# One array for K and V, read in tiles of 7 to 9 places across the borders of K, V and batches

## The chip, the cores and the metric

The kernel runs on one core of a Trainium2 chip. The metric is the device time of one execution in microseconds (us), as a median of runs. The engines named below are TensorE (PE, with PEld for its weight loads), VectorE (DVE), ScalarE (ACT), GpSimd (POOL) and SyncE (SP), which here does nothing but start DMA transfers from HBM to the on-chip memory. Everything is float32.

## The reference

Two rounds of the same pair of layers are applied to 8 batches of one token each: cached attention with 32 query heads on 4 K/V heads, then a GELU network. Both rounds use the same cache and the same weights, so every byte of K, V and the weights is used twice.

```python
B, Sq, D = 8, 1, 1024;  Hq, Hkv, Sk, Dh = 32, 4, 4096, 128;  F = 3584
def _A_ref(x, k_cache, v_cache, wq, wo):
    q = (x @ wq).reshape(B, Sq, Hq, Dh).transpose(0, 2, 1, 3)
    k = jnp.repeat(k_cache, rep, axis=1); v = jnp.repeat(v_cache, rep, axis=1)
    scores = jnp.einsum("bhqd,bhkd->bhqk", q, k) * (Dh ** -0.5)
    o = jnp.einsum("bhqk,bhkd->bhqd", _softmax(scores, axis=-1), v)
    return o.transpose(0, 2, 1, 3).reshape(B, Sq, Hq * Dh) @ wo
def _B_ref(x, w1, b1, w2, b2):
    return jnp.einsum("bsf,fd->bsd", _gelu(jnp.einsum("bsd,df->bsf", x, w1) + b1), w2) + b2
x = A_x
for _ in range(2):
    x = x + _A_ref(_layernorm(x, axis=-1), A_k_cache, A_v_cache, A_wq, A_wo)
    x = x + _B_ref(_layernorm(x, axis=-1), B_w1, B_b1, B_w2, B_b2)
```

## The kernel before

**Memory.** One on-chip tile, the arena, has 52 *places* (`N_UNIT`) of 1024 float32 columns in all 128 partitions, 512 KB each (`SCW`). K of one batch is 16 places, V is 16 places. A transfer fills k neighbouring places from a given first place. The first 28 places hold wq through layer 0, because layer 1's queries are made from the same copy; places 28 to 51 turn over.

**The stream.** All transfers stand in one list, `stream`, in the order in which they will be used, each with its size and its first place written out by hand. `pump` (L272) starts transfers from the head of the list for as long as the places of the next one are free; `release` (L287) frees a tile's places and pumps again. All of them are issued by SyncE on one queue, and a DMA instruction waits, in the program, for the last reader of the places that it overwrites.

```python
def pump():
    while stream:
        key, k, src, starts, keys = stream[0]
        ...
            slot = arena.take(k, [i for i in starts if i + k <= arena.limit])
        if slot is None:
            return
        stream.pop(0)
        nc.sync.dma_start(out=slot.ap[:, 0:src.shape[1]], in_=src)
```

**The order of the work.** Layer 0: wq (q0), then for batch 0 to 7 K and V in tiles of 8 and 4 places; the last V (of batch 7) in pieces of 1, 7, 4 and 4 places, of which the last 15 places stay for layer 1; then wo (o0), w1 (i0) and w2 in tiles of 1 to 4 places. Layer 1 takes the batches as 7, 6, ... 0: K of batch 7 and of batch 6 in small tiles, everything after that in tiles of 8 at places 26, 34 and 18 in turn, then wo (o1: 8, 8, 8, 4, 2, 2), w1 (i1: five of 4, three of 2, then 1, 0.5, 0.5) and the last three pieces of w2 (`LATE`, at place 20).

**The compute.** In `attention`, `scores` (L612) multiplies a pair of places of K with the queries; after 8 pairs `probs` does the softmax with VectorE and ScalarE (L617 to L643); `values` (L657) multiplies the pairs of V, VectorE picks the diagonal blocks (L660, L662), and `heads` (L669) puts the heads in place. `project` (L439) is the product with wo. `expand` (L317, L320) is the product with w1; a unit there is 8 row blocks of 512 columns, which is 4 places, and 7 units make the hidden layer. After half of the first unit it runs the variance of the layer norm (L211, L240), which the scaling of every unit (L335) needs; `hidden_wide` (L413, L417, L429) transposes a unit and applies the GELU. In layer 1 the contraction with w2 (`down_row`, L497) of each unit is woven in behind the next unit's matmuls, and the last thing is the sum on VectorE (L872) and the store.

A transfer's matmuls wait for the whole transfer. Each float32 matmul stands twice in the trace's counts.

Of the kernel before, what the change touches and what calls it, by code (L numbers as in the profile page):

```python
# [21 lines left out]
CH = 512  # L22
# [3 lines left out]
NG = W // CH  # L26
T = CH // P
NR = NH * HKV
EPS = 1e-5
PAD = 24  # L30
SCALE = DH ** -0.5
# [18 lines left out]
        ("w2", 7, 4, 0, 16), ("w2", 8, 4, 16, 8), ("w2", 9, 4, LAST, 4), ("x", 4), ("q", 4, 0), ("q", 4, 1),  # L50
        ("w2", 10, 5, 0, 16), ("q", 5, 0), ("w2", 11, 5, 16, 12), ("q", 5, 1), ("x", 5), ("q", 6, 0),
        ("w2", 11, 6, 0, 4), ("w2", 12, 6, 4, 16), ("q", 6, 1), ("w2", 13, 6, 20, 8), ("x", 6))
LATE_AT = 20
LATE_C = 2
LATE = ((0, 2), (2, 1), (3, 1))
NGR = F // CH
# [56 lines left out]


@with_exitstack
def decode_layers(ctx: ExitStack, tc: tile.TileContext, x, kc, vc, wq, wo, w1, w2, out):


    nc = tc.nc
# [480 lines left out]
    def v_at(b, r):  # L600
        return b, r // NH, r % NH
# [72 lines left out]

    def ap_of(key):

        parts = pieces[st["layer"], key] if (st["layer"], key) in pieces else pieces[0, key]
        chunks = [held[name].ap[:, c:c + CH] for name, c0, n in parts for c in range(c0, c0 + n, CH)]
        return chunks, [name for name, c0, n in parts if c0 + n == held[name].cols]

    def plan(order):

# [64 lines left out]
    def lane(layer, b, a, r, m):
        where = k_at if a == "k" else v_at
        keys = [(a, *where(b, e)) for e in range(r, r + m)]
        for e, key in enumerate(keys):  # L750
            pieces[layer, key] = [((layer, keys[0]), e * W, W)]
        return (layer, keys[0]), (kc if a == "k" else vc)[b][:, r * W:(r + m) * W]

    def cache(layer, b, a, at):
        r = 0
        while r < NR:
            n, starts = at(2 * (NR - r))
            name, src = lane(layer, b, a, r, n // 2)
            yield (name, n, src, starts, ())
            r += n // 2  # L760

    rsum = row_sums()
    nc.vector.tensor_reduce(rsum, x_row, AX.X, ALU.add)

    last_b = B - 1
    shared = (("v7", 1, 44), ("v7b", 7, 28), ("v7c", 4, 35), ("v7d", 4, 39))
    orders = [list(range(B)), list(range(B))[::-1]]

    def fixed(*at):
        return lambda k, i: (at[i],)  # L770
# [8 lines left out]
    def listed(*spots):
        spots = iter(spots)  # L780
        return lambda left: next(spots)

    def batch(layer, b, k_spots, v_spots):
        for a, spots in [(a, spots) for a, spots in (("k", k_spots), ("v", v_spots)) if spots]:
            stream.extend(cache(layer, b, a, listed(*((n, (at,)) for n, at in spots))))
# [3 lines left out]
    batch(0, 0, ((8, 40), (4, 32), (4, 36)), ((4, 28), (8, 40), (4, 32)))
    batch(0, 1, ((4, 36), (4, 28), (8, 40)), ((8, 32), (8, 40)))  # L790
    cycle = [(((8, 36), (4, 44), (4, 28)), ((8, 32), (8, 40))), (((8, 28), (4, 36), (4, 40)), ((4, 44), (8, 28), (4, 36))),
             (((8, 40), (8, 28)), ((4, 36), (8, 40), (4, 28))), (((8, 32), (8, 40)), ((8, 28), (4, 36), (4, 40))),
             (((4, 44), (8, 28), (4, 36)), ((8, 40), (8, 28)))]
    for b in orders[0][2:last_b]:
        batch(0, b, *cycle[(b - 1) % 5])
    batch(0, last_b, cycle[(last_b - 1) % 5][0], ())
    at = 0
    for name, k, to in shared:
        keys = [(1, name, e) for e in range(k)] if at else ()
        stream.append(((0, name), k, vc[last_b][:, at:at + k * SCW], (to,), keys))  # L800
        for e in range(k):
            key = ("v", *v_at(last_b, (at + e * SCW) // W))
            pieces.setdefault((0, key), []).append(((0, name), e * SCW, SCW))
            pieces.setdefault((1, key), []).append(((1, name, e), 0, SCW) if keys else ((1, name), 0, SCW))
        at += k * SCW
    weights(("o0",), wo[0], [3, 2] + [3] * 9, fixed(*[46, 49, 43] * 4))
    weights(("i0",), w1[0], [2] + [3] * 8 + [2], fixed(*[43, 46, 49] * 4))
    down_weights()
    stream.append((("qe", 0), 0, wq[0][:, -W:-KEEP], x_row[:, 0:W - KEEP], ()))
    stream.append(((1, "v7"), 1, vc[last_b][:, 0:SCW], (17,), ()))  # L810
    batch(1, last_b, ((2, 20), (2, 22), (4, 24), (2, 18), (2, 20), (2, 22), (2, 24)), ())
    batch(1, last_b - 1, ((2, 26), (2, 18), (4, 20), (2, 24), (2, 28), (4, 30)), ((8, 34), (8, 18)))
    at = [26, 34, 18] * (4 * B)
    for b in orders[1][2:]:
        batch(1, b, *([(8, at.pop(0)), (8, at.pop(0))] for _ in "kv"))
    weights(("o1",), wo[0], [8, 8, 8, 4, 2, 2], fixed(26, 34, 18, 26, 30, 32))
    weights(("i1",), w1[0], [4] * 5 + [2] * 3 + [1, 0.5, 0.5], fixed(34, 38, 18, 22, 26, 30, 32, 34, 36, 37, 38))
# [7 lines left out]
    for layer in range(2):  # L825
        st["layer"] = layer
        b2_row = spare[:, SCW:SCW + Q4]
        hooks = {("probs", last_b): opened} if layer == 0 else {
            ("v", *v_at(last_b - 2, 0)): lambda: bias_row(b2_row, spare[:, SCW + Q4:SCW + Q4 + CH]),
            ("v", *v_at(last_b - 1, 1)): rebuild,  # L830
            ("v", *v_at(last_b - 3, 0)): bias_diag,
            **{("k", *k_at(last_b, r)): lambda: unread(2) for r in range(NR - 4, NR)}}
        last = attention(orders[layer], hooks)
        rsum = row_sums()
        project(f"o{layer}", oT, x_row, rsum, {4: last})
        rs = layernorm(x_row, rsum)
# [76 lines left out]
def _start(x, b1, b2):  # L913
# [3 lines left out]

_LAYOUT = {
    'x': (('A_x', 'B_b1', 'B_b2'), _start),
    'k': (('A_k_cache',), lambda a: a.reshape(B, HKV, 4, 32, NH, W // DH, DH).transpose(0, 6, 4, 1, 2, 5, 3).reshape(B, P, -1)),  # L920
    'v': (('A_v_cache',), lambda a: a.reshape(B, HKV, P, -1).transpose(0, 2, 1, 3).reshape(B, P, -1)),
    'wq': (('A_wq',), _queries),
    'wo': (('A_wo',), _down),
    'w1': (('B_w1',), _across),
# [24 lines left out]
```

## Time and profile before

| | us |
|---|---|
| median of 3 runs (846.3 to 846.95) | 846.91 |
| profiled execution, whole | 849.2 |
| its span in the trace | 847.3 |
| TensorE busy in the span | 557.7 (66%) |
| VectorE busy | 193.4 (23%) |
| ScalarE busy | 55.9 (7%) |
| share of the 16 DMA engines that SyncE's queue took | 99.0% |

The span is the time from the first to the last instruction in the trace. Busy shares are averages over stages that have different limits, so the stages are read apart. In the chain of work that ended last the page puts 68% on DMA and 28% on TensorE.

### The profile page before, as it was taken

The numbers are of one execution on the slowest core, as the hardware profiler recorded it, in microseconds if no ns is written. First come the engines' busy times: TensorE is split into PE (matmuls) and PEld (weight loads), VectorE is DVE, ScalarE is ACT, GpSimd is POOL, SyncE is SP. The second block draws the span as 40 slices with busy tenths as digits, with TensorE's granted clock in tenths as the row PEclk, the third lists the DMA queues.
The fourth block names the chain that finished last, engine by engine and source line by source line (L and its number), as shares of the span: only waits on it lengthen the run. The fifth ranks groups of instructions, "written<-read, shape, count | busy, mean of one in ns | idle before, by whom it ended". The sixth has DMA issues, their size and how long they took to land.

```text
span 847.3 us, 9962 instructions
## 1 busy us (share of the span) xinstructions
PE 557.7 (66%) x4350; PEld 188.9 (22%) x4350; DVE 193.4 (23%) x642; ACT 55.9 (7%) x118; POOL 2.4 (0%) x14
## 2 busy tenths in 40 slices
PE   0756475566656647688988796576765566665778
PEld 0211121111111112133244322121211111112335
DVE  0013131313223231300010343231314132222011
ACT  0110000000000000000210200000000000000021
POOL 0000000000000000000000000000000000000000
PEclk9977778867787877799999998867688877878679
DMA  9999999999999999999999999999999999999997
GB/s 402 420 424 429 433 422 425 438 425 434 422 430 438 422 439 420 418 414 416 411 407 411 411 409 432 435 429 431 429 433 428 435 431 428 435 425 431 424 425 283
DMA packets 21066, 356.97 MB, mean 421 GB/s; under 512 B 2336, under 2 KB 2720, under 8 KB 4256
## 3 DMA queue, kind: packets, MB, share of 16 engines
q1 hardware_dynamic: 20880, 356.20, 99.0%
q8 instruction: 34, 0.56, 0.3%
q10 hardware_dynamic: 144, 0.15, 0.1%
q14 instruction: 8, 0.07, 0.0%
HBM read 356.21 MB, written 0.13 MB: 421 GB/s over the span
## 4 chain that ended last, share of the span: by engine, by line
DMA 68%; PE 28%; DVE 1%; issue 1%; another core or an unknown queue 1%; ACT 0%; SPq 0%; ACTq 0%; DVEq 0%
DMA arena<-in_k_dram 27%; DMA arena<-in_v_dram 24%; PE sps L612 8%; PE o_ps L657 8%; DMA arena<-in_w_dram 6%; DMA arena<-in_wo_dram 6%; DMA arena<-in_wq_dram 5%; PE acc L376 2%; PE acc L317 2%; PE sps L497 1%; PE y L439 1%; PE sps L484 1%; PE none L195 1%; PE sps L669 1%; PE acc L320 1%
## 5 line engine op out<-in xcount | busy, mean ns | idle before, releaser
L612 PE MATMUL sps<-arena,qz 128*32 128x512 f32 x1024 | 168.7, 801 | 120.2 <-DMA arena<-in_k_dram 119.1
L657 PE MATMUL o_ps<-arena 128*32 128x512 f32 x512 | 88.6, 811 | 44.3 <-DMA arena<-in_v_dram 32.8
L657 PE MATMUL o_ps<-arena,spare 128*32 128x512 f32 x512 | 81.4, 746 | 37.4 <-DMA arena<-in_v_dram 35.1
L612 PEld LDWEIGHTS sps<-arena,qz 128*32 128x32 f32 x1024 | 38.7, 136 | 211.0 <-issue 176.4
L662 DVE SCALAR_TENSOR_TENSOR scr<-o_ps,bits,scr 128x128 f32<-128x128 f32 x192 | 67.4, 351 | 6.8
L660 DVE TENSOR_SCALAR scr<-o_ps,bits 128x128 f32<-128x128 f32 x64 | 22.5, 351 | 135.9 <-PE o_ps L657 135.9
L439 PE MATMUL y<-arena,oxT 128*32 128x256 f32 x512 | 38.4, 444 | 18.1 <-DMA arena<-in_wo_dram 18.1
L669 PEld LDWEIGHTS sps<-bits,scr 128*128 128x128 f32 x128 | 22.0, 216 | 70.1 <-issue 49.1
L376 PE MATMUL acc<-arena,oxT 128*32 128x512 f32 x248 | 33.2, 664 | 6.5 <-DMA arena<-in_wq_dram 4.2
L657 PEld LDWEIGHTS o_ps<-arena 128*32 128x32 f32 x512 | 17.2, 134 | 79.3 <-issue 49.3
L195 PE MATMUL sps<-spare,ident 128*32 128x512 f32 (+2 forms) x82 | 33.9, 533 | 1.1 <-DVE scr L231 0.6
L670 DVE TENSOR_TENSOR oxT<-sps,scr 128x8 f32<-128x8 f32 x64 | 10.6, 165 | 101.1 <-PE sps L669 101.1
L617 DVE TENSOR_SCALAR_CACHE_REDUCE arena<-sps 128x512 f32<-128x512 f32 x16 | 11.1, 692 | 90.8 <-PE sps L612 90.8
L657 PEld LDWEIGHTS o_ps<-arena,spare 128*32 128x32 f32 x512 | 17.2, 125 | 65.4 <-issue 45.4
L638 ACT ACTIVATE sps<-arena,bits 128x512 f32<-128x512 f32 x16 | 10.9, 681 | 283.5 <-DVE scr L632 283.5
L617 DVE TENSOR_SCALAR_CACHE_REDUCE spare<-sps 128x512 f32<-128x512 f32 x16 | 11.1, 692 | 79.8 <-PE sps L612 79.8
L317 PE MATMUL acc<-arena,oxT 128*32 128x512 f32 x160 | 26.7, 675 | 3.8 <-DMA arena<-in_w_dram 3.8
L638 ACT ACTIVATE sps<-spare,bits 128x512 f32<-128x512 f32 x16 | 10.9, 681 | 266.1 <-DVE scr L632 266.1
L669 PE MATMUL sps<-bits,scr 128*128 128x8 f32 x128 | 27.9, 290 | 0.0
L439 PEld LDWEIGHTS y<-arena,oxT 128*32 128x32 f32 x512 | 17.2, 126 | 40.6 <-DMA arena<-in_wo_dram 24.0
L626 PE MATMUL sps<-scr,bits 128*128 128x128 f32 x32 | 7.4, 312 | 21.4 <-DVE scr L622 21.4
L220 PE MATMUL sps<-ident,xb 128*128 128x128 f32 x6 | 1.5, 344 | 24.2 <-DMA xb<-in_x_dram 23.2
(138 smaller groups left out, 285.3 us busy)
## 6 DMA issues: line engine op xcount, KB each, us to landing
arena<-in_v_dram SPq DMA_DIRECT2D x24, 4096.0 KB, 21.9
arena<-in_k_dram SPq DMA_DIRECT2D x22, 4096.0 KB, 21.3
arena<-in_k_dram SPq DMA_DIRECT2D x15, 2048.0 KB, 18.2
arena<-in_v_dram SPq DMA_DIRECT2D x10, 2048.0 KB, 18.6
arena<-in_wo_dram SPq DMA_DIRECT2D x10, 1536.0 KB, 9.8
arena<-in_w_dram SPq DMA_DIRECT2D x10, 1536.0 KB, 8.5
arena<-in_w_dram SPq DMA_DIRECT2D x12, 1024.0 KB, 9.8
arena<-in_w_dram SPq DMA_DIRECT2D x6, 2048.0 KB, 21.9
```

The lines of the kernel that those rows point to most:

```text
L195: nc.tensor.matmul(ps[0:32, 0:w], ident[:, 0:32], ap[:, 0:w], start=True, stop=True)
L317: nc.tensor.matmul(acc[32 * j:32 * j + 32, :], lhs, slot.ap[:, c:c + CH], start=(kt < 4), stop=(kt >= NT - 4))
L376: nc.tensor.matmul(acc[u][32 * j:32 * j + 32, d0 - j * CH:d1 - j * CH], xnT[:, kt * XS:kt * XS + 32], ap[:, d0 - c0:d1 - c0], start=(kt == ...
L439: nc.tensor.matmul(y[32 * j:32 * j + 32, 0:Q4], lhs[:, n * B:n * B + 32], slot.ap[:, c + j * Q4:c + (j + 1) * Q4], start=(n == 0), stop=(n ...
L612: nc.tensor.matmul(ps[32 * g:32 * g + 32, :], qz[:, c:c + 32], kt[g], start=(j == 0), stop=(j == HKV - 1))
L617: nc.vector.tensor_scalar(st["row", b].ap[:, half * CH:(half + 1) * CH], ps, SCALE, None, op0=ALU.mult, op1=ALU.max, accum_out=st["mx", b] ...
L638: nc.scalar.activation(pp, row[:, h * CH:(h + 1) * CH], AF.Exp, bias=bias, scale=1.0, accum_out=ls[:, h:h + 1])
L657: nc.tensor.matmul(o[32 * g:32 * g + 32, :], s[:, g], v[g], start=(half == 0), stop=(half == NH - 1))
L660: nc.vector.tensor_scalar(r, o[:, 0:P], sel_t[:, 0:1], None, op0=ALU.mult)
L662: nc.vector.scalar_tensor_tensor(r, o[:, t * P:(t + 1) * P], sel_t[:, t:t + 1], r, op0=ALU.mult, op1=ALU.add)
L669: nc.tensor.matmul(po[:, 0:REP], r_s[j % 2], sel_h, start=True, stop=True)
L670: nc.vector.tensor_tensor(oT_v[:, j * REP:(j + 1) * REP, b], po[:, 0:REP], rl_s[b % 2][:, j * REP:(j + 1) * REP], ALU.mult)
```

## The change

K and V, before two arrays with a pitch of 64 KB from one partition's row to the next, become one array `kv`: for every batch 16 places of K and 16 of V, all in one row of 256 places per partition, and one place of padding at the end of the row. A tile may hold any run of places, so that it can cross from K to V and from one batch to the next. `ap_of` now looks up the pieces of a pair place by place.

Layer 0 reads tiles of 8, 7 and 8 places at 36, 44 and 28 in turn. Layer 1 takes batch 7 first, as before, and then 0, 1, ... 6; after the small tiles it reads 9, 9 and 8 places at 34, 17 and 26 in turn. o1 is four tiles of 8; i1 is 8, three of 4, three of 2, 1, 0.5 and 0.5; `LATE_AT` goes from 20 to 22. The hooks that rebuild x and lay out the biases stay at the second, third and fourth batch of layer 1's order.

```diff
-LATE_AT = 20
+LATE_AT = 22
...
-        parts = pieces[st["layer"], key] if (st["layer"], key) in pieces else pieces[0, key]
-        chunks = [held[name].ap[:, c:c + CH] for name, c0, n in parts for c in range(c0, c0 + n, CH)]
-        return chunks, [name for name, c0, n in parts if c0 + n == held[name].cols]
+        parts = [part for _, part in sorted(pieces[st["layer"], key].items())]
+        chunks = [held[name].ap[:, c + e:c + e + CH] for name, c in parts for e in range(0, SCW, CH)]
+        return chunks, [name for name, c in parts if c + SCW == held[name].cols]
...
+    def cache(layer, g, spots, part=None):
+
+        for k, at in spots:
+            name = (layer, "kv", g)
+            keys = [(1, "kv", g + e) for e in range(k)] if part else ()
+            stream.append((name, k, kv[:, g * SCW:(g + k) * SCW], (at,), keys))
...
+            g += k
+        return g
...
-    orders = [list(range(B)), list(range(B))[::-1]]
+    orders = [list(range(B)), [last_b, *range(last_b)]]
...
+    low, mid, high = (8, 28), (8, 36), (7, 44)
+    g = cache(0, 0, [mid, high, low] * 10 + [mid, (2, 46)])
+    g = cache(0, g, ((1, 44),))
+    cache(0, g, ((7, 28), (4, 35), (4, 39)), part=True)
...
-    at = [26, 34, 18] * (4 * B)
-    for b in orders[1][2:]:
-        batch(1, b, *([(8, at.pop(0)), (8, at.pop(0))] for _ in "kv"))
-    weights(("o1",), wo[0], [8, 8, 8, 4, 2, 2], fixed(26, 34, 18, 26, 30, 32))
-    weights(("i1",), w1[0], [4] * 5 + [2] * 3 + [1, 0.5, 0.5], fixed(34, 38, 18, 22, 26, 30, 32, 34, 36, 37, 38))
+    low, mid, high = (9, 17), (8, 26), (9, 34)
+    cache(1, 0, [(2, 26), (2, 18), (4, 20), (2, 24), (2, 28), (4, 30), high, low] + [mid, high, low] * 7 + [mid])
+    weights(("o1",), wo[0], [8] * 4, fixed(34, 17, 26, 34))
+    weights(("i1",), w1[0], [8] + [4] * 3 + [2] * 3 + [1, 0.5, 0.5], fixed(17, 26, 30, 34, 38, 40, 17, 19, 20, 21))
...
+def _cache(k, v):
+    import numpy as _np
+    k = k.reshape(B, HKV, 4, 32, NH, W // DH, DH).transpose(0, 6, 4, 1, 2, 5, 3).reshape(B, P, -1)
+    v = v.reshape(B, HKV, P, -1).transpose(0, 2, 1, 3).reshape(B, P, -1)
+    rows = _np.concatenate([k, v], 2).transpose(1, 0, 2).reshape(P, -1)
+    return _np.concatenate([rows, _np.zeros((P, SCW), _np.float32)], 1)
```

SyncE's queue at the start of the cache reads of layer 0, before (columns of a transfer; 8192 are 8 places):

```order
L282 DMA arena<-in_k_dram 128x8192
L282 DMA arena<-in_k_dram 128x4096 x2
L282 DMA arena<-in_v_dram 128x4096
L282 DMA arena<-in_v_dram 128x8192
L282 DMA arena<-in_v_dram 128x4096
L282 DMA arena<-in_k_dram 128x4096 x2
L282 DMA arena<-in_k_dram 128x8192
L282 DMA arena<-in_v_dram 128x8192 x2
```

The same place in the program now:

```order
L283 DMA arena<-in_kv_dram 128x8192
L283 DMA arena<-in_kv_dram 128x7168
L283 DMA arena<-in_kv_dram 128x8192 x2
L283 DMA arena<-in_kv_dram 128x7168
L283 DMA arena<-in_kv_dram 128x8192 x2
```

Eleven transfers for two batches became eight and a part of a ninth, and only the first of a batch begins where K begins.

SyncE's queue at the end of layer 1, before (the last of V, wo, w1, then the late pieces of w2, which the rows also call in_w_dram):

```order
L282 DMA arena<-in_v_dram 128x8192 x2
L282 DMA arena<-in_wo_dram 128x8192 x3
L282 DMA arena<-in_wo_dram 128x4096
L282 DMA arena<-in_wo_dram 128x2048 x2
L282 DMA arena<-in_w_dram 128x4096 x5
L282 DMA arena<-in_w_dram 128x2048 x3
```

And now:

```order
L283 DMA arena<-in_kv_dram 128x8192
L283 DMA arena<-in_wo_dram 128x8192 x4
L283 DMA arena<-in_w_dram 128x8192
L283 DMA arena<-in_w_dram 128x4096 x3
L283 DMA arena<-in_w_dram 128x2048 x3
```

The last three tiles of wo became one, and the first two of w1 became one.

TensorE at the start of layer 1's expansion, before, with the semaphores that a row waits for (DMAHW is a transfer's):

```order
L317 MATMUL acc<-arena,oxT 32x512 [waits DMAHW3_49,DVE_49,PE_49]
L317 MATMUL acc<-arena,oxT 32x512 x3
L211 MATMUL sps<-bits 32x1 [waits Activation_49]
L211 MATMUL sps<-bits 32x1 x3
L317 MATMUL acc<-arena,oxT 32x512 x4
L413 MATMUL sps<-ident,scr 128x128 [waits Activation_49]
L413 MATMUL sps<-ident,scr 128x128 x3
L317 MATMUL acc<-arena,oxT 32x512 [waits DMAHW4_49]
L317 MATMUL acc<-arena,oxT 32x512 x7
```

And now:

```order
L318 MATMUL acc<-arena,oxT 32x512 [waits DMAHW7_49,DVE_49,PE_49]
L318 MATMUL acc<-arena,oxT 32x512 x3
L212 MATMUL sps<-bits 32x1 [waits Activation_49]
L212 MATMUL sps<-bits 32x1 x3
L318 MATMUL acc<-arena,oxT 32x512 x4
L414 MATMUL sps<-ident,scr 128x128 [waits Activation_49]
L414 MATMUL sps<-ident,scr 128x128 x3
L318 MATMUL acc<-arena,oxT 32x512 x8
```

The matmuls and their order are the same to the end; the wait that stood ahead of unit 1 (DMAHW4) is gone, since both units lie in the transfer that the first row waits for.

## Rows read from the trace of the kernel before

**Rows 1.** The page: DMA share by slice in tenths; SyncE's queue (packets, MB, share).
```profile
DMA  9999999999999999999999999999999999999997
...
q1 hardware_dynamic: 20880, 356.20, 99.0%
```

**Rows 2.** Stages: us; busy PE, PEld, DVE, ACT, POOL; granted clock, DMA share, GB/s.
```profile
50.00:330.00 280.00, 168.55 (x990) 47.03 (x994) 72.75 (x237) 10.63 (x28) 0.00 (x0) 0.76 1.00 429
...
530.00:775.00 245.00, 149.68 (x886) 43.55 (x885) 69.11 (x223) 9.11 (x24) 0.00 (x0) 0.78 1.00 431
...
810.00:820.00 10.00, 8.73 (x68) 2.85 (x72) 0.88 (x4) 3.55 (x7) 0.00 (x0) 0.58 1.00 421
820.00:840.00 20.00, 19.55 (x344) 12.26 (x340) 2.67 (x11) 3.21 (x8) 0.00 (x0) 1.00 0.99 406
```

**Rows 3.** Timeline, last stage: start, us, engine, line, operation, [idle before <-releaser].
```profile
810.42 1.94 PE L317 MATMUL acc<-arena,oxT 128*32 128x512 f32 x8 [2.62 <-DMA arena<-in_w_dram]
...
812.10 0.32 PE L211 MATMUL sps<-bits 128*32 128x1 f32 x8
...
812.51 0.26 ACT L240 ACTIVATE bits<-sps,bits 128x1 f32<-128x1 f32 x1 [2.31 <-PE sps L211]
...
814.28 0.69 ACT L335 ACTIVATE scr<-acc,bits 128x512 f32<-128x512 f32 x1
...
815.02 1.12 PE L413 MATMUL sps<-ident,scr 128*128 128x128 f32 x4 [0.85 <-ACT scr L335]
...
816.07 3.01 PE L317 MATMUL acc<-arena,oxT 128*32 128x512 f32 x16
...
818.91 1.90 PE L497 MATMUL sps<-arena,oxT 128*32 128x256 f32 x32
...
820.74 0.66 PE L413 MATMUL sps<-ident,scr 128*128 128x128 f32 x4
...
822.16 1.92 PE L317 MATMUL acc<-arena,oxT 128*32 128x512 f32 x16
...
844.17 0.42 DVE L872 TENSOR_TENSOR xb<-xb,sps 128x256 f32<-128x256 f32 x1 [2.32 <-PE sps L497]
```

**Rows 4.** Waits from 785 to 847 us: us in total, times, longest.
```profile
PE acc L317 <- DMA arena<-in_w_dram: 2.6, 1, 2.6
...
PE sps L253 <- DVE qz L417: 0.5, 1, 0.5
```

**Rows 5.** Timeline of TensorE, arrivals of 8-place tiles of wo in layer 1.
```profile
776.12 2.50 PE L439 MATMUL y<-arena,oxT 128*32 128x256 f32 x32 [3.71 <-DMA arena<-in_wo_dram]
...
785.84 6.18 PE L439 MATMUL y<-arena,oxT 128*32 128x256 f32 x64 [4.03 <-DMA arena<-in_wo_dram]
795.57 9.02 PE L439 MATMUL y<-arena,oxT 128*32 128x256 f32 x112 [3.55 <-DMA arena<-in_wo_dram]
```

**Rows 6.** Timeline of TensorE, arrivals of 3-place tiles in layer 0, first and last of six.
```profile
379.67 1.50 PE L439 MATMUL y<-arena,oxT 128*32 128x256 f32 x24 [0.49 <-DMA arena<-in_wo_dram]
...
398.14 1.50 PE L439 MATMUL y<-arena,oxT 128*32 128x256 f32 x24 [0.50 <-DMA arena<-in_wo_dram]
```

**Rows 7.** DMA of 50 to 330 us, then of 530 to 775 us: queue; issues, us to landing.
```profile
q1 hardware_dynamic: 5484, 119.88, 100.1%
...
arena<-in_v_dram SPq DMA_DIRECT2D x10, 4096.0 KB, 18.7
...
q1 hardware_dynamic: 3620, 105.38, 100.0%
...
arena<-in_v_dram SPq DMA_DIRECT2D x12, 4096.0 KB, 23.6
```

**Rows 8.** Timeline, layer 0, batch 1: end of K, softmax, first tile of V.
```profile
102.61 6.46 PE L612 MATMUL sps<-arena,qz 128*32 128x512 f32 x32 [7.89 <-DMA arena<-in_k_dram]
...
113.25 3.64 PE L657 MATMUL o_ps<-arena 128*32 128x512 f32 x16 [2.30 <-DVE arena L639]
...
117.39 2.49 PE L657 MATMUL o_ps<-arena 128*32 128x512 f32 x16
```

More of the change, by code (lines that the diff above doesn't have):

```diff
@@ L28 @@
 NR = NH * HKV
+RU = 2 * NR
 EPS = 1e-5
@@ L115, in decode_layers @@
 @with_exitstack
-def decode_layers(ctx: ExitStack, tc: tile.TileContext, x, kc, vc, wq, wo, w1, w2, out):
+def decode_layers(ctx: ExitStack, tc: tile.TileContext, x, kv, wq, wo, w1, w2, out):
     nc = tc.nc
@@ L745, in weights @@
             at += n
[L747 to L760, printed above, removed]
+    def cache(layer, g, spots, part=None):
[3 more added lines that the diff above has]
+            stream.append((name, k, kv[:, g * SCW:(g + k) * SCW], (at,), keys))
+            for e in range(k):
+                b, r = divmod(g + e, 2 * RU)
+                a, r = "kv"[r // RU], r % RU // 2
+                key = (a, *(k_at if a == "k" else v_at)(b, r))
+                pieces.setdefault((layer, key), {})[g + e] = name, e * SCW
+                if part:
+                    pieces.setdefault((1, key), {})[g + e] = keys[e], 0
+            g += k
+        return g
     rsum = row_sums()
@@ L765, in decode_layers @@
     last_b = B - 1
-    shared = (("v7", 1, 44), ("v7b", 7, 28), ("v7c", 4, 35), ("v7d", 4, 39))
-    orders = [list(range(B)), list(range(B))[::-1]]
+    orders = [list(range(B)), [last_b, *range(last_b)]]
     def fixed(*at):
@@ L777, in down_weights @@
             c0 += cols
[L779 to L785, printed above, removed]
     halves = lambda i: [[("q", kt, u) for kt in kts for u in range(2)] for kts in ((0, 1, 2, 3), (4, 5), (6,), ())][i]
     weights(("q0",), wq[0], [16, 8, 4, 4], fixed(0, 16, 24, 28), kept=halves)
[L789 to L805, printed above, removed]
+    low, mid, high = (8, 28), (8, 36), (7, 44)
+    g = cache(0, 0, [mid, high, low] * 10 + [mid, (2, 46)])
+    g = cache(0, g, ((1, 44),))
+    cache(0, g, ((7, 28), (4, 35), (4, 39)), part=True)
     weights(("o0",), wo[0], [3, 2] + [3] * 9, fixed(*[46, 49, 43] * 4))
@@ L809, in decode_layers @@
     stream.append((("qe", 0), 0, wq[0][:, -W:-KEEP], x_row[:, 0:W - KEEP], ()))
-    stream.append(((1, "v7"), 1, vc[last_b][:, 0:SCW], (17,), ()))
-    batch(1, last_b, ((2, 20), (2, 22), (4, 24), (2, 18), (2, 20), (2, 22), (2, 24)), ())
-    batch(1, last_b - 1, ((2, 26), (2, 18), (4, 20), (2, 24), (2, 28), (4, 30)), ((8, 34), (8, 18)))
-    at = [26, 34, 18] * (4 * B)
-    for b in orders[1][2:]:
-        batch(1, b, *([(8, at.pop(0)), (8, at.pop(0))] for _ in "kv"))
-    weights(("o1",), wo[0], [8, 8, 8, 4, 2, 2], fixed(26, 34, 18, 26, 30, 32))
-    weights(("i1",), w1[0], [4] * 5 + [2] * 3 + [1, 0.5, 0.5], fixed(34, 38, 18, 22, 26, 30, 32, 34, 36, 37, 38))
+    first = last_b * 2 * RU
+    cache(1, first + RU, ((1, 17),))
+    cache(1, first, ((2, 20), (2, 22), (4, 24), (2, 18), (2, 20), (2, 22), (2, 24)))
+    low, mid, high = (9, 17), (8, 26), (9, 34)
+    cache(1, 0, [(2, 26), (2, 18), (4, 20), (2, 24), (2, 28), (4, 30), high, low] + [mid, high, low] * 7 + [mid])
+    weights(("o1",), wo[0], [8] * 4, fixed(34, 17, 26, 34))
+    weights(("i1",), w1[0], [8] + [4] * 3 + [2] * 3 + [1, 0.5, 0.5], fixed(17, 26, 30, 34, 38, 40, 17, 19, 20, 21))
     for e, n in LATE:
@@ L828, in decode_layers @@
         hooks = {("probs", last_b): opened} if layer == 0 else {
-            ("v", *v_at(last_b - 2, 0)): lambda: bias_row(b2_row, spare[:, SCW + Q4:SCW + Q4 + CH]),
-            ("v", *v_at(last_b - 1, 1)): rebuild,
-            ("v", *v_at(last_b - 3, 0)): bias_diag,
+            ("v", *v_at(orders[1][2], 0)): lambda: bias_row(b2_row, spare[:, SCW + Q4:SCW + Q4 + CH]),
+            ("v", *v_at(orders[1][1], 1)): rebuild,
+            ("v", *v_at(orders[1][3], 0)): bias_diag,
             **{("k", *k_at(last_b, r)): lambda: unread(2) for r in range(NR - 4, NR)}}
@@ L919 @@
     'x': (('A_x', 'B_b1', 'B_b2'), _start),
-    'k': (('A_k_cache',), lambda a: a.reshape(B, HKV, 4, 32, NH, W // DH, DH).transpose(0, 6, 4, 1, 2, 5, 3).reshape(B, P, -1)),
-    'v': (('A_v_cache',), lambda a: a.reshape(B, HKV, P, -1).transpose(0, 2, 1, 3).reshape(B, P, -1)),
+    'kv': (('A_k_cache', 'A_v_cache'), _cache),
     'wq': (('A_wq',), _queries),
```

## The prediction

> **What bounds the kernel now.** I read the slices of the page first. The 16 DMA engines are busy for nine tenths or more of every slice but the last, and the one queue that SyncE fills takes 99.0% of them with 20880 packets [rows 1]. A transfer is 128 packets of data, one per partition, and 16 that count the semaphore up, so 20880 / 144 = 145 transfers. TensorE is busy 66% of the span, so up to its last stage the kernel goes at the pace of the queue, and I ask two things: what a transfer costs beyond its bytes, and where the queue stops being the limit.
>
> The table by stage answers the second. In the middle of both layers TensorE works 60% of the time; from 820 to 840 us it works 19.55 of 20 us [rows 2]. That is the last stage, the expansion of layer 1 (w1) with the contraction (w2) woven in. Its rows show how it starts: TensorE waits 2.62 us for the first w1 tile, begins at 810.42, and sums half a unit (a unit is 4 places, 8 row blocks). Behind that, on its own queue, come the variance matmuls (812.10), then ScalarE's root (812.51) and scaled copy (814.28), and at 815.02 the transposes of unit 0 [rows 3]. From there to the last matmul, which ends just before VectorE's sum at 844.17, each row starts where the one before ends. The waits of this stage say the same: one wait of TensorE's matmuls for a w1 transfer, 2.6 us, the one at 810.42, and one of 0.5 us for VectorE [rows 4]. So the end is set by **when the first w1 tile has landed**, plus 844.17 - 810.42 = 33.75 us of work in a fixed order. The later w1 tiles are there in time.
>
> **What a transfer costs.** Where TensorE waits for every tile, its starts are landings. Tiles of 8 places start work at 776.12, 785.84 and 795.57: 9.72 us apart [rows 5]. Tiles of 3 places start at 379.67 and, five tiles later, at 398.14: 18.47 / 5 = 3.694 us [rows 6]. With p per place and o per transfer, 8p + o = 9.72 and 3p + o = 3.694, so p = 1.205 us and o = 0.08 us. The other bound is the rate of whole stages: 5484 packets (38.1 transfers) moved 119.88 MB in 280 us in layer 0, 3620 (25.1) moved 105.38 MB in 245 us in layer 1 [rows 7]. At layer 1's rate layer 0's bytes would take 278.7 us; the 1.3 us more belong to 38.1 - 28.6 = 9.5 more transfers than layer 1's size would need, 0.14 us each. I take 0.08, because it comes from single tiles, and keep 0.14.
>
> **The change, part by part.**
>
> *Fewer transfers.* 132 for 145; 8 fewer in the cache reads of layer 0, 2 in those of layer 1, 2 in o1 and 1 where the first two tiles of w1 become one. All 13 go ahead of the point that counts for the end, the landing of unit 1: 13 x 0.08 = **-1.0 us** (to -1.8 at 0.14). The bytes are the same.
>
> *Borders crossed, three tiles in turn.* A tile now frees its places when its last place is used, and a tile can hold the end of K and the start of V, with the softmax between them. TensorE took 6.46 us for 8 places of K at the slow clock, began V 4.2 us after the last of them, and was through 8 places of V at 119.8, some 6.5 us later [rows 8]. Half of each gives 3.2 + 4.2 + 3.3 = 10.7 us of holding. The tile that takes its place is due on the engines when the two between have landed: 15 places x 1.205 = 18.1 us in layer 0, 17 x 1.205 = 20.5 us in layer 1. So there are some 7 us to spare, and transfers that are issued 18.7 us (layer 0) and 23.6 us (layer 1) ahead of landing today stay well ahead [rows 7]. Cost **0**; if that cover went, the queue would run dry at one tile per batch.
>
> *One array, another row pitch.* Rows of a partition lie 257 x 4 KB apart instead of 64 KB. The trace has pitches of 64 KB (K, V) and 128 KB (wo): in rows 5 wo tiles arrive at the pace of the cache tiles of rows 2 (4.19 MB / 9.72 us = 431 GB/s). No row shows a pitch near 1 MB. I take **0**, from the nearest rows, with a loss kept as a rival; a gain is left out since 64 KB and 128 KB run alike. The Trainium skill (DMA: Bandwidth & Descriptors, Latency and other measured facts) speaks against long pitches: copies at 512 KB and 2 MB ran slower, and 4 KB of padding on a pitch gave the full rate back. By that rule the padded pitch of this array costs nothing; by its figures for bare pitches (207 and 164 GB/s where 214 is full) the 608 us of cache reads would grow by 20 us and more, an estimate from that page. No run here shows either yet.
>
> *Order of batches.* 7, 0, 1, ... for 7, 6, 5, ...: the same bytes and instructions, hooks at the same positions. 0.
>
> *The first w1 tile.* It was 4 places and is 8. SyncE's and TensorE's rows in the change show it: the first wait in the expansion is for the whole 8 places, and unit 1 has no wait of its own any more. The queue hands over 4 more places before TensorE may begin: 4 x 1.205 = **+4.8 us**. What could hide it? The chain up to 815.02 sits behind the first half unit on TensorE and goes with it. The rest is the same rows in the same order with one wait of 0.5 us, so nothing gives the time back. o1's last tile grows from 2 places to 8, but its matmuls (64 rows took 6.18 us [rows 5]) and the layer norm end within the 9.7 us that the w1 tile needs. The transfers behind land earlier than TensorE wants them. o1's first two tiles are used before the tail's places are needed, so the queue doesn't stall.
>
> **Sum.** 4.8 - 1.0 = **+3.8 us**. The profiled execution took 849.2 us, 847.3 of them span, and would take 853.0; it lay 2.3 us above the median of the runs. Carried to the median: 846.9 + 3.8 = **850.7 us**.
>
> **Rivals.**
>
> 1. *The clock comes up earlier or the start is partly absorbed.* At 810 to 820 the granted clock averages 0.58, then 1.00 [rows 2]: 8 matmul rows took 1.94 us and 16 took 3.01, where 16 later took 1.92; the transposes 1.12 and then 0.66 [rows 3]. On the path that is 1.0 + 0.5 + 1.1 = 2.6 us. Now the o1 burst comes shortly ahead, and if the stage ran at 2.4 GHz from the start the time would be 850.7 - 2.6 = 848.1 us. Against it: the three bursts of o1 were also followed by waits and did not leave the engine at 2.4 GHz at 810.
> 2. *The clock comes up later.* A mean of 0.58 over those 10 us is 8.4 us at 1.2 GHz and then 2.4; a unit more at 1.2 GHz costs 0.8 + 1.9 us: 853.4 us.
> 3. *Faster: the queue, not TensorE, sets the end.* If the 33.75 us had 4.8 us of slack, through waits that the matmul rows don't show, the end would follow the last transfer; at 0.14 us each that is 846.9 - 1.8 = 845.1 us. It decides as soon as the work behind 815.02 shrinks to the time the queue needs. Against it: 19.55 of 20 us busy.
> 4. *The cache reads slow down,* by the new pitch or by a tile held over 18 us. The cache is 260.6 MB, 608 us at 429 GB/s; each per cent costs 6 us: 857 us at 1%; from half a per cent on it outweighs the rest of the sum's doubt.
>
> That the change does not do what it says is not open: the order rows show 132 transfers and the 8-place first tile.
>
> **How the numbers follow.** Forecast 0.56 (849.2 to 852.2), rival 1 0.17, rival 2 0.09, rival 3 0.10, rival 4 0.08. The predicted time is 850.7. The range leaves out rivals 3 and 4 and reaches to the others, with room below rival 1 for 0.14 us per transfer: 847.0 to 853.4. A measurement of this kernel tells 0.2% (1.7 us) from no change: slower means over 848.6, faster under 845.2. Slower: 0.56 + 0.09 + 0.08 and 0.03 of rival 1 = 0.76; the same 0.14; faster 0.10.
>
> **What would show it.** Right: 19008 packets (132 x 144) on SyncE's queue; tiles of 9 places 10.9 us apart; the first matmul of the last expansion starts some 4 us later in the span, after a longer wait for w1; no wait for w1 behind it; the queue is empty some 4 us before TensorE ends; a stage rate of 430 to 431 GB/s in both layers. Wrong: the cache stages below 428 GB/s (rival 4); matmul rows of units 0 and 1 at 1.92 us per 16 (rival 1); an expansion that ends less than 33 us after its first tile without a clock change (rival 3).

## The result and the profile after

| | before | after |
|---|---|---|
| median, us | 847.39 (22 runs, 845.77 to 851.27) | 850.46 (22 runs, 848.63 to 855.85) |
| ratio to before | | 1.0036, 95% interval 1.0024 to 1.0049 |
| span of the profiled execution, us | 847.3 | 850.4 |

The change makes the kernel 0.36% slower, 3.1 us (2.0 to 4.2). In the two profiled executions the difference of the spans is 3.1 us as well. The traces are laid side by side below; a part of their agreement with the medians is chance, as the section on why the prediction was right shows.

The page of after (DMA share by slice in tenths, SyncE's queue) and its stages (us; busy PE, PEld, DVE, ACT, POOL; granted clock, DMA share, GB/s):

```profile
DMA  9999999999999999999999999999999999999994
...
q1 hardware_dynamic: 19008, 356.20, 98.5%
```

```profile
50.00:330.00 280.00, 175.83 (x994) 46.31 (x994) 72.68 (x237) 10.63 (x28) 0.00 (x0) 0.77 1.00 431
530.00:775.00 245.00, 148.65 (x893) 39.87 (x896) 68.94 (x223) 9.11 (x24) 0.00 (x0) 0.81 1.00 431
810.00:820.00 10.00, 6.68 (x48) 2.53 (x52) 1.96 (x8) 4.45 (x8) 0.00 (x0) 0.59 1.00 426
820.00:840.00 20.00, 19.55 (x293) 10.96 (x289) 2.16 (x9) 3.67 (x8) 0.00 (x0) 0.95 0.93 379
840.00:851.00 11.00, 7.13 (x168) 4.70 (x160) 1.25 (x4) 0.46 (x2) 0.00 (x0) 0.92 0.04 15
```

There are 19008 / 144 = 132 transfers with the same bytes as in [rows 1]. The cache reads run at 431 GB/s in both layers, where [rows 2] had 429 and 431: neither the row pitch nor the tiles across the borders slow the queue. The last slice falls from 7 tenths to 4: from 840 us on, the DMA engines have nothing left to do (0.04 of the time, 15 GB/s), while TensorE works on for 7.13 us. So the queue is empty some 7 us before TensorE's last matmul ends (847.1), and the end is TensorE's. Before, it was some 2 us: the DMA share was 0.47 from 841 to 842 us and 0.04 in the next, and the last matmul ended at 844.1.

The timeline of TensorE in after, from the first tile of wo (start, us, engine, line, operation, [idle before <-releaser]), and VectorE's last sum:

```profile
783.96 5.35 PE L440 MATMUL y<-arena,oxT 128*32 128x256 f32 x64 [3.89 <-DMA arena<-in_wo_dram]
793.67 5.35 PE L440 MATMUL y<-arena,oxT 128*32 128x256 f32 x64 [4.36 <-DMA arena<-in_wo_dram]
803.39 6.10 PE L440 MATMUL y<-arena,oxT 128*32 128x256 f32 x64 [4.37 <-DMA arena<-in_wo_dram]
...
810.54 0.24 PE L212 MATMUL sps<-bits 128*32 128x1 f32 x8
813.20 1.94 PE L318 MATMUL acc<-arena,oxT 128*32 128x512 f32 x8 [2.41 <-DMA arena<-in_w_dram]
...
817.80 1.12 PE L414 MATMUL sps<-ident,scr 128*128 128x128 f32 x4 [0.85 <-ACT scr L336]
818.85 3.48 PE L318 MATMUL acc<-arena,oxT 128*32 128x512 f32 x16
822.15 1.90 PE L498 MATMUL sps<-arena,oxT 128*32 128x256 f32 x32
```

```profile
847.20 0.42 DVE L851 TENSOR_TENSOR xb<-xb,sps 128x256 f32<-128x256 f32 x1 [2.32 <-PE sps L498]
```

The second tile of wo lands at 783.96 instead of 785.84 [rows 5], 1.88 us earlier. From there the first w1 matmul is 813.20 - 783.96 = 29.24 us away; before it was 810.42 - 785.84 = 24.58 [rows 3, 5]. That is 4.66 us more, and 4 more places with 3 transfers fewer are 4.82 - 0.24 = 4.58 by the unit prices. So the first matmul starts 2.78 us later. Behind it the work takes 847.20 - 813.20 = 34.0 us, 33.75 before: one row of 16 matmuls took 3.48 instead of 3.01 us while the clock was still low, and 0.2 us of that came back in later rows.

The waits of after from 785 to 851 us (engine, line, what for: us in total, times, longest):

```profile
PE acc L318 <- DMA arena<-in_w_dram: 2.4, 1, 2.4
...
PE sps L254 <- DVE qz L418: 0.5, 1, 0.5
```

As in [rows 4] there is one wait for w1, the first. The stage has no other place where it could give the later start back.

### The profile page after: what moved, and what is told of

Same layout as the page of the kernel before. It is cut to its first block, busy times and chain, and to the rows that moved or that the text cites. A ratio compares the mean times of both kernels' runs of the same rounds, so it can differ in the third digit from the quotient of the medians.

```text
span 850.4 us, 9902 instructions
## 1 busy us (share of the span) xinstructions
PE 561.6 (66%) x4350; PEld 184.4 (22%) x4350; DVE 193.2 (23%) x642; ACT 55.9 (7%) x118; POOL 2.4 (0%) x14
## 3 DMA queue, kind: packets, MB, share of 16 engines
q1 hardware_dynamic: 19008, 356.20, 98.5%
## 4 chain that ended last, share of the span: by engine, by line
DMA 63%; PE 31%; DVE 3%; ACT 1%; issue 1%; SPq 0%; ACTq 0%; DVEq 0%
DMA arena<-in_kv_dram 44%; PE o_ps L658 10%; DMA arena<-in_wo_dram 8%; DMA arena<-in_w_dram 7%; PE sps L613 7%; DMA arena<-in_wq_dram 5%; PE acc L377 2%; PE acc L318 2%; PE y L440 1%; PE sps L498 1%; PE sps L485 1%; PE none L196 1%; ACT sps L639 1%; PE sps L670 1%; PE sps L627 1%
## 5 line engine op out<-in xcount | busy, mean ns | idle before, releaser
L613 PE MATMUL sps<-arena,qz 128*32 128x512 f32 x1024 | 175.2, 772 | 115.2 <-DMA arena<-in_kv_dram 114.1
L658 PE MATMUL o_ps<-arena 128*32 128x512 f32 x512 | 84.5, 739 | 39.8 <-DMA arena<-in_kv_dram 23.6
L613 PEld LDWEIGHTS sps<-arena,qz 128*32 128x32 f32 x1024 | 36.0, 133 | 215.6 <-DMA arena<-in_kv_dram 126.7
L639 ACT ACTIVATE sps<-arena,bits 128x512 f32<-128x512 f32 x16 | 10.9, 681 | 284.3 <-DVE scr L633 284.3
L639 ACT ACTIVATE sps<-spare,bits 128x512 f32<-128x512 f32 x16 | 10.9, 681 | 271.8 <-DVE scr L633 271.8
```

Source lines behind the costliest of these rows:

```text
L613: nc.tensor.matmul(ps[32 * g:32 * g + 32, :], qz[:, c:c + 32], kt[g], start=(j == 0), stop=(j == HKV - 1))
L639: nc.scalar.activation(pp, row[:, h * CH:(h + 1) * CH], AF.Exp, bias=bias, scale=1.0, accum_out=ls[:, h:h + 1])
L658: nc.tensor.matmul(o[32 * g:32 * g + 32, :], s[:, g], v[g], start=(half == 0), stop=(half == NH - 1))
```

## The experiments

The question is whether the 8-place first tile of w1 explains the whole difference, whether the cache reads gain or lose anything, and what the clock does with it. Each ratio is to the kernel before on the same chips.

**The first tile alone, taken back.** After, with i1 in the sizes of before:

```diff
-    weights(("i1",), w1[0], [8] + [4] * 3 + [2] * 3 + [1, 0.5, 0.5], fixed(17, 26, 30, 34, 38, 40, 17, 19, 20, 21))
+    weights(("i1",), w1[0], [4] * 5 + [2] * 3 + [1, 0.5, 0.5], fixed(17, 21, 26, 30, 34, 38, 40, 17, 19, 20, 21))
```

> The changed kernel with one thing undone: the w1 tiles of layer 1 are five of 4 places again instead of one of 8 and three of 4 (places 17, 21, 26, 30, 34, ...). Theory (the end is the landing of the first w1 tile plus some 34 us of TensorE work): the first matmul of the last expansion starts 4 x 1.205 = 4.8 us earlier than in the changed kernel, one transfer more costs 0.08 us behind it, so the time is 850.5 - 4.8 = 845.7 us, if the clock behaves alike; with the before kernel at 847.4 the ratio to before is 0.998. Rival (the loss comes from the cache reads, the new row pitch or tiles that are held too long): the time stays near 850.5, ratio 1.0036.

Measured: 847.46 us (12 runs), ratio 0.9995 (0.9976 to 1.0014). The loss is gone. The gain of 0.2% that I had expected on top does not show, though the interval does not exclude it. TensorE in this kernel:

```profile
803.08 5.18 PE L440 MATMUL y<-arena,oxT 128*32 128x256 f32 x64 [4.94 <-DMA arena<-in_wo_dram]
808.82 0.44 PE L221 MATMUL sps<-ident,xb 128*128 128x128 f32 x2 [0.57 <-DVE xb L454]
...
809.95 1.06 PE L318 MATMUL acc<-arena,oxT 128*32 128x512 f32 x8 [0.39 <-PE sps L212]
```

The first w1 row waits for the layer norm (0.39 us, released by TensorE's own L212), no longer for a DMA. By the unit prices the 4-place tile landed at 803.08 + 4.82 + 0.08 = 808.0, when the last 8-place tile of wo was still being multiplied (to 808.3). So the merge of o1's last tiles, which delayed nothing in after, delays TensorE's start by 2.0 us once the first w1 tile is small again.

**The first tile alone, put into before.** Before, with i1 starting with 8:

```diff
-    weights(("i1",), w1[0], [4] * 5 + [2] * 3 + [1, 0.5, 0.5], fixed(34, 38, 18, 22, 26, 30, 32, 34, 36, 37, 38))
+    weights(("i1",), w1[0], [8] + [4] * 3 + [2] * 3 + [1, 0.5, 0.5], fixed(34, 18, 22, 26, 30, 32, 34, 36, 37, 38))
```

> The kernel before with only the first two w1 tiles of layer 1 made one of 8 places (at place 34). Theory: the last expansion begins 4.8 us later, and the time is 847.4 + 4.8 = 852.2 us, ratio 1.0057. Rival (the queue sets the end, or the loss is in the cache reads): 847.4 us, ratio 1.000.

Measured: 851.32 us (10 runs), ratio 1.0037 (1.0015 to 1.0058): the loss of the whole change, from this one edit. The 3.1 us are less than the 4.8 us that I had priced, but the interval (1.3 to 4.9 us) reaches that far. TensorE:

```profile
815.01 1.94 PE L317 MATMUL acc<-arena,oxT 128*32 128x512 f32 x8 [6.19 <-DMA arena<-in_w_dram]
...
819.50 0.66 PE L413 MATMUL sps<-ident,scr 128*128 128x128 f32 x4 [0.91 <-ACT scr L335]
820.09 1.92 PE L317 MATMUL acc<-arena,oxT 128*32 128x512 f32 x16
```

The start is 815.01 - 810.42 = 4.6 us later in the span, about as priced; counted from the second tile of wo, which landed at 785.13 here, it is 5.3 us later. But the transposes (0.66 for 1.12 us) and the next 16 matmuls (1.92 for 3.01) already ran at the higher clock: 1.5 us came back there. That the later start or the longer idle time brought this is not shown: the kernel with split cache tiles below has the tail of before and an idle time of 2.63 us, and its clock rose just as soon.

**The first tile made larger still.** After, with 12 places:

```diff
-    weights(("i1",), w1[0], [8] + [4] * 3 + [2] * 3 + [1, 0.5, 0.5], fixed(17, 26, 30, 34, 38, 40, 17, 19, 20, 21))
+    weights(("i1",), w1[0], [12] + [4] * 2 + [2] * 3 + [1, 0.5, 0.5], fixed(17, 30, 34, 38, 40, 17, 19, 20, 21))
```

> The changed kernel with the first w1 tile of layer 1 made of 12 places for 8 (at place 17; then two of 4). Theory: 4 more places before TensorE may begin, 4 x 1.205 = 4.8 us on top of 850.5: 855.3 us, ratio 1.0093; less by what the clock gives back (two units and a half arrive at once). Rival (the loss does not hang on this tile): 850.5 us.

Measured: 856.17 us (4 runs, 853.38 to 856.56), ratio 1.0094 (1.0064 to 1.0125). In its profiled execution, the shortest of the four, TensorE idles 8 us for the tile:

```profile
816.39 1.93 PE L318 MATMUL acc<-arena,oxT 128*32 128x512 f32 x8 [8.00 <-DMA arena<-in_w_dram]
```

With 4, 8 and 12 places in otherwise the same kernel the ratios are 0.9995, 1.0036 and 1.0094: 3.5 us and 4.9 us a step, each uncertain by 2 to 3 us, where 4 places take 4.8 us on the queue. In the traces the first matmul comes 34.07 us behind the second tile of wo (816.39 - 782.32) with 12 places and 29.24 with 8: 4.8 us for the step. With 4 places it comes 2.0 us after its tile has landed (above), so that step moves the start by less.

**The cache reads alone.** After, with o1 and i1 in the sizes of before, so that the one array, the tiles across borders, the order of the batches and the place of the late w2 pieces are left:

```diff
-    weights(("o1",), wo[0], [8] * 4, fixed(34, 17, 26, 34))
-    weights(("i1",), w1[0], [8] + [4] * 3 + [2] * 3 + [1, 0.5, 0.5], fixed(17, 26, 30, 34, 38, 40, 17, 19, 20, 21))
+    weights(("o1",), wo[0], [8, 8, 8, 4, 2, 2], fixed(34, 17, 26, 34, 38, 40))
+    weights(("i1",), w1[0], [4] * 5 + [2] * 3 + [1, 0.5, 0.5], fixed(17, 21, 26, 30, 34, 38, 40, 17, 19, 20, 21))
```

> The changed kernel with the tail of the kernel before: wo of layer 1 in 8, 8, 8, 4, 2, 2 and w1 in five tiles of 4 places first; so the cache part of the change alone. In the run with only w1 undone TensorE started the expansion 2.5 us after w1 had landed, behind the 8 places of wo that it still had to multiply. Theory: with wo in small pieces it starts at the landing again, some 10 transfers x 0.08 us earlier than in the kernel before: 847.4 - 0.8 = 846.6 us, ratio 0.999. Rival (the cache part costs time by itself): 848.5 us or more, ratio over 1.001.

Measured: 847.84 us (12 runs), ratio 0.9997 (0.9980 to 1.0015): no difference from before that can be measured, so a loss over 0.15% is excluded for the cache part, and a gain of more than 0.2% too. The 0.8 us that I had expected is too little to be told (the 2.5 us in the expectation are the 2.0 us above). TensorE:

```profile
808.44 1.94 PE L318 MATMUL acc<-arena,oxT 128*32 128x512 f32 x8 [1.36 <-DMA arena<-in_w_dram]
...
814.08 3.36 PE L318 MATMUL acc<-arena,oxT 128*32 128x512 f32 x16
```

TensorE starts at the landing of the w1 tile again, 24.62 us behind the second tile of wo (783.82), as before (24.58).

**What a transfer costs.** Before, with each 8-place tile of layer 1's last six batches as two of 4, 24 more transfers:

```diff
-        batch(1, b, *([(8, at.pop(0)), (8, at.pop(0))] for _ in "kv"))
+        batch(1, b, *([(4, s + d) for s in (at.pop(0), at.pop(0)) for d in (0, 4)] for _ in "kv"))
```

> The kernel before with the cache tiles of layer 1's last six batches split from 8 into two of 4 places at the same places: 24 transfers more. It measures what a transfer costs in a full queue. By single landings 0.08 us each: 847.4 + 1.9 = 849.3 us, ratio 1.0023, and 429 GB/s at 530 to 775 us. By whole stages 0.14 each: 850.8 us, ratio 1.004. If a transfer cost its fixed time in a row, 24 x 2 us: 895 us.

Measured: 849.33 us (10 runs), ratio 1.0008 (0.9989 to 1.0027), +0.7 us (-0.9 to 2.3). That is 0.03 us per transfer, 0.10 at most. The queue from 530 to 775 us in this kernel (packets, MB, share; before in [rows 7]), the landings of layer 1's first large tile of V and of the second tile of wo, and before's first large tile of V:

```profile
q1 hardware_dynamic: 7010, 104.81, 100.6%
```

```profile
518.81 3.64 PE L657 MATMUL o_ps<-arena,spare 128*32 128x512 f32 x16 [5.33 <-DMA arena<-in_v_dram]
784.36 5.35 PE L439 MATMUL y<-arena,oxT 128*32 128x256 f32 x64 [3.67 <-DMA arena<-in_wo_dram]
```

```profile
522.12 3.21 PE L657 MATMUL o_ps<-arena,spare 128*32 128x512 f32 x16 [5.21 <-DMA arena<-in_v_dram]
```

Twice the packets in that stretch move 104.81 MB instead of 105.38; at 430 GB/s that is 1.3 us for the 23.5 more transfers in it, 0.06 us each. The landings tell it better. From the one tile to the other it took 784.36 - 518.81 = 265.55 us, before 785.84 - 522.12 = 263.72: 1.83 us for 24 transfers with the same bytes, 0.076 us each. The price of 0.08 us holds; 0.14 does not. That the tile of wo landed 1.5 us earlier than in [rows 5] comes from ahead of layer 1's cache reads, where this execution was 3.3 us earlier already, with the same program.

TensorE at the last expansion of this kernel, whose tail is that of before:

```profile
809.65 1.93 PE L317 MATMUL acc<-arena,oxT 128*32 128x512 f32 x8 [2.63 <-DMA arena<-in_w_dram]
...
814.14 0.66 PE L413 MATMUL sps<-ident,scr 128*128 128x128 f32 x4 [1.00 <-ACT scr L335]
814.73 1.92 PE L317 MATMUL acc<-arena,oxT 128*32 128x512 f32 x16
...
824.25 1.92 PE L317 MATMUL acc<-arena,oxT 128*32 128x512 f32 x16 [0.28 <-DMA arena<-in_w_dram]
...
829.16 1.93 PE L317 MATMUL acc<-arena,oxT 128*32 128x512 f32 x16 [0.63 <-DMA arena<-in_w_dram]
```

Behind the same idle time as before (2.63 and 2.62 us) the transposes and the next 16 matmuls ran at the higher clock, and TensorE then waited twice for later tiles of w1.

**The pitch without its padding.** After, with rows of exactly 1 MB (256 places of 4 KB):

```diff
-    return _np.concatenate([rows, _np.zeros((P, SCW), _np.float32)], 1)
+    return rows
```

> The changed kernel without the one place of padding, so that the rows of two partitions lie exactly 1 MB apart; everything else alike. Theory that only the 4 KB of padding keep the cache reads at full rate: the cache stages fall under 420 GB/s, and each per cent costs 6 us (at 3%, 870 us). Rival (the queue's engines set the rate and the pitch doesn't matter): 850.5 us and 431 GB/s in both cache stages, as in the changed kernel.

Measured: 854.06 us (10 runs), ratio 1.0063 (1.0039 to 1.0088). Its stages:

```profile
50.00:330.00 280.00, 174.59 (x1004) 46.32 (x1004) 72.93 (x238) 10.63 (x28) 0.00 (x0) 0.79 1.00 430
530.00:775.00 245.00, 158.06 (x911) 42.28 (x906) 69.72 (x224) 9.11 (x24) 0.00 (x0) 0.76 1.00 431
```

The bare pitch reads at 430 and 431 GB/s. The difference from after is 0.27%, 2.3 us, and the two intervals overlap; by the medians the padding is worth between nothing and some 5 us. The landings put nearly all of that outside the cache reads. Here are the first tiles of K and of wo in layer 0 and the first large tile of V and the second tile of wo in layer 1 with the bare pitch, and then the first three of these in after (its second tile of wo is at 783.96, above):

```profile
53.50 5.85 PE L613 MATMUL sps<-arena,qz 128*32 128x512 f32 x32 [5.24 <-DMA arena<-in_kv_dram]
...
360.69 1.50 PE L440 MATMUL y<-arena,oxT 128*32 128x256 f32 x24 [1.46 <-DMA arena<-in_wo_dram]
...
523.37 3.64 PE L658 MATMUL o_ps<-arena,spare 128*32 128x512 f32 x16 [7.02 <-DMA arena<-in_kv_dram]
...
785.74 4.97 PE L440 MATMUL y<-arena,oxT 128*32 128x256 f32 x64 [3.16 <-DMA arena<-in_wo_dram]
```

```profile
53.44 5.61 PE L613 MATMUL sps<-arena,qz 128*32 128x512 f32 x32 [4.83 <-DMA arena<-in_kv_dram]
...
360.10 1.50 PE L440 MATMUL y<-arena,oxT 128*32 128x256 f32 x24 [1.46 <-DMA arena<-in_wo_dram]
...
521.60 3.63 PE L658 MATMUL o_ps<-arena,spare 128*32 128x512 f32 x16 [6.55 <-DMA arena<-in_kv_dram]
```

From the one tile to the other it takes 307.19 us in layer 0 with the bare pitch and 306.66 with the padding, in layer 1 262.37 and 262.36. So in these two traces the padding is worth some 0.5 us there. The rest of the 2.3 us is not shown to belong to the pitch. The Trainium skill (DMA: Bandwidth & Descriptors, Latency and other measured facts) lists copies at pitches of 512 KB and 2 MB at 207 and 164 GB/s where 214 is full. Reads into on-chip memory with rows of 28 to 36 KB did not lose like that here, and the measurement decides for this kernel.

**The clock of the last stage.** After, with three matmuls whose result nobody reads (six in the trace's count), ahead of the expansion, in the idle time before the first w1 tile:

```diff
+            idle(*[CH] * 3)
             expand("i1", rs, work)
```

> The changed kernel with three matmuls of 512 columns, whose result nobody reads, put on TensorE between layer 1's layer norm and its last expansion, where it waits 2.4 us for w1. Theory (the work behind the first w1 tile is bound by TensorE, part of it at 1.2 GHz): if the granted clock rises a few us earlier, up to 2.6 us go: 848 to 850.5 us. Rival (TensorE is not the limit there): no change with the clock, 850.5 us. If the clock does not rise earlier, the run tells nothing.

Measured: 849.66 us (10 runs), ratio 1.0020 (0.9997 to 1.0043). TensorE, and the stage from 810 to 820 us:

```profile
810.15 2.76 PE L196 MATMUL sps<-spare,ident 128*32 128x512 f32 x6 [0.61 <-DVE scr L232]
812.68 1.08 PE L318 MATMUL acc<-arena,oxT 128*32 128x512 f32 x8
...
816.94 1.93 PE L318 MATMUL acc<-arena,oxT 128*32 128x512 f32 x16
```

```profile
810.00:820.00 10.00, 8.19 (x78) 2.89 (x82) 1.40 (x6) 5.03 (x9) 0.00 (x0) 1.00 0.99 419
```

The granted clock is 1.00 (2.4 GHz) where after had 0.59, and 16 matmuls take 1.93 instead of 3.48 us. From the first w1 row to the end of the span it takes 847.5 - 812.68 = 34.8 us instead of 850.4 - 813.20 = 37.2. So the low clock costs 2.4 us in the profiled execution of after. By the medians the fill brings 1.4 us, and the intervals overlap.

**Both: the cache alone, with the fill.** The kernel of the cache reads alone, and the three unread matmuls:

> The cache part alone, with three unread matmuls of 512 columns ahead of the last expansion. Theory (the last stage is TensorE's, partly at 1.2 GHz): the clock is at 2.4 GHz for the first units and up to 2.6 us go, until the last w2 pieces set the end (they land some 1.7 us before TensorE ends in the kernel before): 845 us, ratio 0.997. Rival (the queue sets the end once w1's first tile is small): as without the fill, 846.6 us.

Measured: 848.42 us (12 runs), ratio 1.0013 (0.9991 to 1.0035): no gain that can be measured; the 0.3% of my expectation lies outside the interval. TensorE and its last stage:

```profile
822.87 1.92 PE L318 MATMUL acc<-arena,oxT 128*32 128x512 f32 x16 [0.54 <-DMA arena<-in_w_dram]
...
827.77 1.92 PE L318 MATMUL acc<-arena,oxT 128*32 128x512 f32 x16 [0.63 <-DMA arena<-in_w_dram]
```

```profile
820.00:840.00 20.00, 18.36 (x359) 12.41 (x348) 2.28 (x9) 3.18 (x8) 0.00 (x0) 1.00 0.93 378
```

TensorE started at 808.19 and at the high clock, and now it waits for later tiles of w1, as the kernel with the split cache tiles did. In the chain of work that ended last the transfers of w1 now reach up to 827.73 us, and TensorE's matmuls follow without another wait of theirs for a transfer: with a small first tile and the clock up, the queue is the limit again. Counted from the second tile of wo (783.71 here), the span ends after 61.4 us, and before it ended after 61.5 (847.3 - 785.84), with the clock still low at the start of the stage. So before, too, the queue was close behind TensorE, and there was little to be gained from either side. No version was measurably faster than before.

## Why the prediction was right

**The first w1 tile, +4.8 us: right in mechanism and, in the trace, in size.** Its own tile moved the first matmul 4.6 us in the kernel that had this edit alone, and 4.66 us against the second tile of wo in after, with three transfers fewer on the way; the step from 8 to 12 places moved it 4.8 us. The median shows less in the kernel with this edit alone, 3.1 us, but its interval (1.3 to 4.9) does not exclude 4.8. In its trace 1.5 us came back because the clock rose sooner. This is rival 1, and I had spoken against it: a part of it occurs, though not in the profiled execution of after, and it occurs without a longer wait too, in the kernel with split cache tiles. In what share of the executions of before and after it occurs, the mean clocks do not tell, and that stays open.

**Fewer transfers, -1.0 us: the price held, but the trace showed 1.88 us by the second tile of wo.** The cache reads have 10 transfers fewer by then, 0.8 us at 0.08. In layer 0 this can be read off, with the kernel that has only the first w1 tile changed standing for before, whose own first tile of wo nobody waited for:

```profile
53.55 6.68 PE L612 MATMUL sps<-arena,qz 128*32 128x512 f32 x44 [4.87 <-DMA arena<-in_k_dram]
...
360.84 1.50 PE L439 MATMUL y<-arena,oxT 128*32 128x256 f32 x24 [1.45 <-DMA arena<-in_wo_dram]
```

These are 307.29 us, after 306.66: 0.6 us for 8 transfers. Two more in layer 1 are 0.15 us at 0.076. The other 1.1 us arise where the change leaves the transfers as they were. Some 0.4 lie ahead of the first tile of K (53.82 before, 53.44 after), and, by subtraction, the rest in the weights of layer 0: from the first tile of wo to layer 1's first large tile of V, the six kernels with the padded array took from 159.6 to 161.5 us with the same program. By the medians, too, the cache reads alone gave no more than 0.9997 (0.9980 to 1.0015), so 13 transfers are less than a measurement of this kernel can tell. The upper price of 0.14 us, from the rates of two stages, was wrong.

**Borders, pitch, order of the batches, 0: right.** 431 GB/s in both stages, and 0.9997 (0.9980 to 1.0015) for the three together with the fewer transfers. Tiles of 9 places took 10.9 us as expected: in after two tiles of layer 1's cache start at 616.75 and 627.68.

```profile
616.75 1.51 PE L658 MATMUL o_ps<-arena,spare 128*32 128x512 f32 x8 [4.38 <-DMA arena<-in_kv_dram]
627.68 6.06 PE L613 MATMUL sps<-arena,qz 128*32 128x512 f32 x36 [3.95 <-DMA arena<-in_kv_dram]
```

**The cover of o1's last tile: right.** It ends within the time that the 8-place w1 tile needs (TensorE still waits 2.41 us). In the kernel with a 4-place tile behind it that cover is gone, and TensorE starts 2.0 us after the tile has landed. I had left this out of that kernel's expectation. What it costs in time is not shown: without the merge the ratio was 0.9997, with it 0.9995, while their clocks differed (16 matmuls in 3.36 and in 1.92 us).

**The rivals.** Rival 3 (the queue sets the end) is refuted for after: one wait for w1, and 7 us of TensorE's work with idle DMA engines. It does occur once the work behind the first w1 row shrinks, as I had said: in the kernel with the cache alone and the fill, and in the one with split cache tiles, TensorE waits for later tiles of w1. Rival 4 (slow cache reads) is refuted by the stage rates. Rival 2 (the clock a unit later) was not seen in full: 16 matmuls took 3.48 us instead of 3.01, and the next 16 took 1.93, as before. The price of rival 1, 2.6 us for the whole low clock, was about right: the fill brought 2.4 us in the trace.

**The sum.** +3.8 us were forecast, 3.1 (2.0 to 4.2) measured. That the forecast of 850.7 us stands beside 850.46 is in part luck: the three runs of before that I started from had a median of 846.91, all 22 one of 847.39, and the difference came out 0.7 lower. In the trace the parts are 4.66 instead of 4.58 for the tile and its three transfers, -1.88 instead of -0.8 for the ten, +0.25 instead of 0 behind the start: 3.0 together. Without the 1.1 us that arise where no transfer was changed they would be 4.1, at the upper end of the measured interval; what makes the medians differ by less, executions with an earlier clock or mere scatter, is not shown. Two signs were off: the first matmul started 2.78 us later in the span and not 4, by the same 1.1 us, and the queue was empty some 7 us before TensorE ended and not 4, since it had been empty some 2 us before the end already.

## What to carry to other kernels

Where the last stage is bound by an engine, look at the transfer that starts it: here each place that was added to it put the start off by its whole time on the queue, 1.2 us, and one transfer less gave 0.08 us back. So look first for the one merge whose landing someone waits for. And when such a wait is taken away, look at what it covered: here a merged tile of the stage before, and, with the clock up as well, the queue itself. When two executions are laid side by side, measure from landing to landing in each stretch: the stretch that no edit touched scattered by 2 us here, and those of the cache reads by a few tenths at most.

## What was not expected of the hardware

- Rows at a pitch of exactly 1 MB read at 430 to 431 GB/s, as fast as at 64 KB; by the landings of one trace each the padding place is worth some 0.5 us in 570 us of reads.
- 24 transfers more, of 2 MB in place of 4 MB, cost 1.83 us between the same two landings of a full queue, 0.076 us each, and 0.7 us (-0.9 to 2.3) by the medians.
- With one and the same order of matmuls, the time from the first w1 row to the end of the span differs by the clock, apart from 0.2 us: 36.9 us before (847.3 - 810.42) and 37.2 in after, but 35.0 in before with the 8-place tile (850.0 - 815.01) and 35.1 with 12 places (851.5 - 816.39), where the clock rose sooner. TensorE had idled for 6.19 and 8.00 us there, but the idle time alone does not decide it: with 2.63 us in the kernel with split cache tiles the clock rose as soon, with 2.62 us before it did not. Each kernel has one trace, and why it rose sooner is not settled.
